# A two-part kernel on one core: VectorE takes attention taps in pairs, and a second input is loaded in four pieces

## The chip, the cores and the metric

The program runs on one core of a Trainium2 chip. A core has engines that work side by side, each with its own queue of instructions, taken strictly in order: TensorE (PE; weight loads are listed apart as PEld), VectorE (DVE), ScalarE (ACT), GpSimd (POOL) and SyncE (SP), which here issues nearly all DMAs. The engines wait for each other through semaphores. SBUF is the working memory of 128 partitions, PSUM takes the results of TensorE. The metric is the device time of one execution, in microseconds (us); less is better.

## The reference

Two independent computations on (1, 2048, 448) bf16 inputs, their results side by side in an output of (1, 2048, 896). Part A is a diagonal complex state-space model with 448 states, part B is windowed attention with 16 heads of 28, in which each token looks at itself and at 7 earlier tokens at distances of 2, 4, ... 14.

```python
# A
Lam_bar = jnp.exp(dt * Lam)
B_bar = ((Lam_bar - 1.0) / Lam)[:, None] * Bmat
Bu = jnp.einsum("bld,pd->blp", x + 0j, B_bar)
for t in range(L):
    h = Lam_bar[None, :] * h + Bu[:, t, :]
    hs.append(h)
y = 2.0 * jnp.einsum("blp,dp->bld", hseq, Cmat).real + x * Dskip[None, None, :]
# B, W = 8, dil = 2
qkv = x @ wqkv
kg, vg = k[:, :, idx_c, :], v[:, :, idx_c, :]     # idx = pos - 2 * [0..7]
logits = jnp.einsum("bhsd,bhswd->bhsw", q, kg) * scale     # masked where idx < 0
attn = softmax(logits)
out = einsum("bhsw,bhswd->bhsd", attn, vg) @ wo
```

## The kernel before

**Layout.** 2048 positions are 128 chunks of 16 consecutive tokens: partition p holds chunk p, and "token j" (0 to 15) stands for 128 positions at once. All work is per token j.

**Part B.** x is loaded from the last tokens to the first. For each j TensorE transposes x (`pt_x`), ScalarE copies that out into `xT` (which lies in the memory that `vd` takes later), and TensorE projects to q, k or v (`qkv_ps`, 4 matmuls of 448 columns each); ScalarE or VectorE evicts it to `qd`, `kd`, `vd`. `kd` and `vd` have 14 halo rows in front, which SyncE fills by copies from the partition before (`_halo`), with zeros for the first chunk (`_zero`). The logits are made by VectorE in two blocks b of 8 tokens (b = 1, tokens 8-15, first). For each of 8 taps w it multiplies `qd` by the shifted `kd` (`prod`, 3584 elements a partition), adds the upper half of the 28 head elements to the lower (`prod` again, 1792) and once more (`sd`, 896). TensorE then sums the remaining 7 slices with 7 identity matmuls into `lg_ps`; after 4 taps ScalarE copies them to `logits`. The softmax has a `top` on VectorE (the maximum), a subtraction on TensorE, an exponential on ScalarE and a `bottom` on VectorE. Then P.V on VectorE, in three blocks of tokens (8-15, 0-5, 6-7): per tap a product of `attn` with the shifted `vd` and an add into one of two sums. Each token's sums are transposed by TensorE (`pt_o`), copied by ScalarE (`oT_sb`), multiplied by `wo` (`wo_ps`), copied (`yb`) and stored.

**Part A.** B_bar is turned into `Bcat` by TensorE and ScalarE. x of A is loaded, transposed (`pt_x`, line 751) and kept in `xaT_sb`. Level 1 is a recurrence over the 16 tokens in two halves, `l1A` and `l1B`, on TensorE with an eviction by ScalarE behind each step; the states go out to `hs` in DRAM. Level 2 is a chain of 7 steps over the 128 chunks (line 829), again TensorE and ScalarE in turn. Then `ga`, and for each token the corrections `coA`, `coB` and the output `y_ps` (4 matmuls at line 902, 7 at line 907).

**Order.** Nothing is ordered by hand. Each piece of work is a unit with an engine, a cost, dependences and a priority; `Planner.run` simulates the engines with these costs, starts at each point the unit that can start earliest (ties by priority), and writes the instructions out in that order. So the order on each engine is fixed when the program is built, and a unit that is late on the chip holds up all that stand behind it on its engine. Some units may go to either of two engines (evictions of projections to ScalarE, or to VectorE at a handicap `HAND`). `acq` and `rel` name buffers that a unit takes and gives back: 4 PSUM banks `mm`, 2 `pt`, 2 `lg`, `SD` buffers `sd`.

B's x and then A's x lie in one place, tag `xin`: the first load of A's x can only be issued when all 16 transposes of B have been read. V of tokens 0 to `VH` - 1 is held: its projections may not start before the last step of `l1A`.

Of the kernel before, what the change touches and what calls it, by code (L numbers as in the profile page):

```python
# [15 lines left out]
D = 448  # L16
# [20 lines left out]
SD = 2  # L37
VH = 8
PVP = (4, 5, 6)
WIDE = set()  # L40
# [8 lines left out]
def act(n):  # L49
    return n / 1200.0 + 0.06  # L50
# [6 lines left out]
def vec2(n):  # L57
    return n / 1920.0 + 0.15
# [85 lines left out]
class PartB:  # L144
    JG = (3, 2, 1, 0)
    HAND = (0.5, 1.0, 1.0)
    PV = ((1, 8, 16, "xin", 2), (0, 0, 6, "qd", 2), (0, 6, 8, "lg", 2))
# [6 lines left out]
    def loads(self):  # L154
        nc, pool, P = self.nc, self.pool, self.plan
        self.x_sb = pool.tile([NCH, T, D], bf16, name="xb_sb", tag="xin")
# [5 lines left out]
        def xload(j0, j1):  # L162
            nc.sync.dma_start(self.x_sb[:, j0:j1], xv[:, j0:j1])
# [22 lines left out]
    def alloc(self):  # L186
# [6 lines left out]
        self.zsrc = pool.tile([1, DH * H], bf16, name="zsrc")  # L193
        V.memset(self.zsrc[:], 0.0)
# [45 lines left out]
    def prep(self):  # L240
# [4 lines left out]
        self.lgb, self.lps = {}, {}  # L245
        self.attn = None
        P.add("SP", 0.1, lambda: self._zero(self.kd), prio=0)
        for g in self.JG:
            if g < 3 and g > 0:
                self.q_proj(range(4 * g + 4, 4 * g + 8), 0)  # L250
            for j in range(4 * g + 3, 4 * g - 1, -1):
                box = {}

                def tr(j=j, box=box):
                    pt = box["pt"] = self.psum.tile([KP, KT, NCH], bf16, name="pt_x", tag="pt")
                    for k in range(KT):
                        nc.tensor.transpose(pt[:, k, :], self.x_sb[:, j, k * KP:(k + 1) * KP], self.ident[:])
# [44 lines left out]
    def qk(self, b, prio):  # L302
# [4 lines left out]
        for w in range(W):  # L307
            o = HALO + j0 - DIL * w

            nd = 14 if (b, w) in WIDE else 7  # L310

            def mul(w=w, o=o, i0=0, i1=JB):
                if "pr" not in box:
                    box["pr"] = pool.tile([NCH, DH, JB, H], bf16, name="prod", tag="prod")
                V.tensor_tensor(box["pr"][:].rearrange("p d j h -> p j d h")[:, i0:i1], self.qd[:, j0 + i0:j0 + i1],  # L315
                                self.kd[:, o + i0:o + i1], op=ALU.mult)

            split = b == 1 and w == 0

            def prod(w=w, o=o, nd=nd, split=split, mul=mul):  # L320
                mul(i0=0, i1=HB if split else JB)
                pr = box.pop("pr")
                prf = pr[:].rearrange("p d j h -> p d (j h)")
                sd = box[w] = pool.tile([NCH, nd, BH], bf16, name="sd", tag="sd", bufs=SD)
                if nd == 14:
                    V.tensor_tensor(sd[:], prf[:, 0:14], prf[:, 14:28], op=ALU.add)
                else:
                    V.tensor_tensor(prf[:, 0:14], prf[:, 0:14], prf[:, 14:28], op=ALU.add)  # L328
                    V.tensor_tensor(sd[:], prf[:, 0:7], prf[:, 7:14], op=ALU.add)  # L329

            def summ(w=w, nd=nd):
                if w % 4 == 0:
                    box["lps"] = self.psum.tile([NCH, 4, BH], f32, name="lg_ps", tag="lg")
                for d in range(nd):
                    nc.tensor.matmul(box["lps"][:, w % 4, :], lhsT=self.ident[:], rhs=box[w][:, d, :],  # L335
                                     start=(w % 4 == 0 and d == 0), stop=(d == nd - 1), skip_group_check=True)
                if w % 4 == 3 and (b, w // 4) in self.maskrow:
                    nc.tensor.matmul(box["lps"][:].rearrange("p w (j h) -> p w j h", h=H), lhsT=self.ident[:],
                                     rhs=self.maskrow[b, w // 4].unsqueeze(3).to_broadcast([NCH, 4, JB, H]),
                                     start=False, stop=True, skip_group_check=True)  # L340

            def evict(w=w):
                if w == 3:
# [3 lines left out]
                nc.scalar.copy(self.lgb[b][:, w - 3:w + 1, :], box["lps"][:])  # L347
            deps = [self.u_q[j] for j in range(j0, j0 + JB)]
            deps += [self.u_kh[p] if p < HALO else self.u_k[p - HALO] for p in range(o, o + JB)]
            cost = vec2(3584) + vec2(1792) + (vec2(896) if nd == 7 else 0.0)  # L350
            if split:
                cost -= vec2(1792) - 0.15
                deps = [P.add("DVE", vec2(1792), lambda mul=mul: mul(i0=HB), deps[HB:JB] + deps[JB + HB:], prio)] + deps
            u = P.add("DVE", cost, prod, deps, prio, acq="sd", lat=0.15 if w % 4 == 3 else 0.8)
            ds.append(u)
            sums.append(P.add("PE", pe(nd, 128) + (0.21 if w % 4 == 3 else 0.0), summ, [u] + sums[-1:], 2, rel="sd",
                              acq="lg" if w % 4 == 0 else None))
            if w % 4 == 3:
# [666 lines left out]
```

## Time and profile before

| | |
|---|---|
| time, median of 3 runs | 163.42 us (162.52 to 164.99) |
| the profiled execution | 163.71 us, its span 161.9 us |
| TensorE busy | 153.8 us (95% of the span), 1748 matmuls |
| VectorE busy | 141.8 us (88%), 156 instructions |
| ScalarE busy | 118.8 us (73%), 242 instructions |
| DMA engines busy | 46% (main queue) |
| granted TensorE clock | 0.996 of full speed |

The span runs from the first instruction to the last on the core; the execution's own time has 1.8 us more around it. Busy time counts the whole length of an instruction, and matmuls overlap, so a busy TensorE isn't TensorE at its peak. In a timeline each row has the start, the length, the engine, the line of the kernel, the operation, and what it writes and reads; a bracket at its end gives the time that the engine was idle before it and who released it. Line numbers are those of the kernel before.

### The profile page before, as it was taken

Reading aid. Unit: us, or ns where it says so; the run is one execution under the profiler, and the core shown is the slowest. Engines: PE = TensorE matmul, PEld = TensorE weight load, DVE = VectorE, ACT = ScalarE, POOL = GpSimd, SP = SyncE. Lnnn points to the kernel's source line nnn. Section 1 sums busy time; section 2 is a strip of 40 time slices with the busy share of each in tenths; the row PEclk is TensorE's granted clock in tenths of the full one; section 3 lists DMA queues with packets and bytes.
Section 4 is the critical chain, followed back from the end, with each engine's and each line's share of the span. In section 5 each row is a group of like instructions: output and inputs, shape, how many; then the busy total and the mean of one; then the engine's idle time right before and its main releaser. Section 6 shows DMA issues by size and latency. Waiting matters only on the chain.

```text
span 161.9 us, 4322 instructions
## 1 busy us (share of the span) xinstructions
PE 153.8 (95%) x1748; PEld 116.5 (72%) x1748; DVE 141.8 (88%) x156; ACT 118.8 (73%) x242; POOL 4.8 (3%) x36
## 2 busy tenths in 40 slices
PE   7998999999999899998999899999999999999991
PEld 7655575767999798998997556677776676786760
DVE  1479999999999999999999999999999999999800
ACT  3497899999976778555557799856657686676862
POOL 5004000000000020000000000000000000000000
PEclk9999999999999999999999999999999999999998
DMA  5999233596875623122222440755543334511312
GB/s 156 327 304 222 61 112 91 158 332 148 117 133 184 174 93 110 63 89 84 89 85 59 136 116 5 218 168 156 167 120 114 113 106 125 170 59 61 115 59 85
DMA packets 24147, 21.39 MB, mean 132 GB/s; under 512 B 9259, under 2 KB 22469, under 8 KB 24127
## 3 DMA queue, kind: packets, MB, share of 16 engines
q1 hardware_dynamic: 24056, 21.11, 46.0%
q8 instruction: 13, 0.21, 0.6%
q14 instruction: 7, 0.06, 0.1%
q10 hardware_dynamic: 71, 0.01, 0.0%
HBM read 10.56 MB, written 7.34 MB: 111 GB/s over the span
## 4 chain that ended last, share of the span: by engine, by line
PE 50%; DVE 33%; ACT 13%; issue 2%; DVEq 0%; ACTq 0%
DVE prod L315 16%; PE y_ps L907 13%; PE qkv_ps L221 10%; DVE prod L328 9%; PE wo_ps L451 7%; DVE sd L329 5%; PE pt_o L441 5%; ACT vd L260 3%; PE warm L963 2%; ACT kd L229 2%; PE coA L884 2%; PE coA L886 2%; PE y_ps L902 2%; ACT Bcat L728 2%; ACT pbuf L834 2%; PE coB L884 2%
## 5 line engine op out<-in xcount | busy, mean ns | idle before, releaser
L221 PE MATMUL qkv_ps<-wqkv_nat,vd 112*128 112x448 bf16 x192 | 41.4, 355 | 1.1 <-ACT vd L260 0.7
L315 DVE TENSOR_TENSOR prod<-qd,kd 128x3584 bf16<-128x3584 bf16 (+1 forms) x17 | 32.5, 1912 | 0.7
L221 PEld LDWEIGHTS <-vd 112*128 112x128 bf16 x192 | 17.8, 98 | 15.0 <-issue 1.6
L794 PEld LDWEIGHTS <-Bcat 112*128 112x128 bf16 x448 | 26.6, 98 | 1.1
L425 DVE TENSOR_TENSOR acc<-acc,pv_tmp 128x3584 bf16<-128x3584 bf16 (+2 forms) x18 | 25.2, 1402 | 0.6
L424 DVE TENSOR_TENSOR pv_tmp<-attn,vd 128x3584 bf16<-128x3584 bf16 (+2 forms) x18 | 25.2, 1400 | 0.4
L907 PE MATMUL y_ps<-Ccat,ht 128*128 128x448 bf16 x112 | 24.5, 352 | 0.0
L328 DVE TENSOR_TENSOR prod<-prod 128x1792 bf16<-128x1792 bf16 x16 | 17.5, 1092 | 0.5
L794 PE MATMUL l1A<-xaT_sb,Bcat 112*128 112x128 bf16 x256 | 16.9, 219 | 0.0
L912 ACT CAST ya<-y_ps 128x448 bf16<-128x448 f32 x16 | 8.5, 532 | 10.2 <-PE y_ps L907 7.7
L907 PEld LDWEIGHTS <-ht 128*128 128x128 bf16 x112 | 10.0, 97 | 6.8
L805 ACT CAST ht<-l1A 128x512 bf16<-128x512 f32 x15 | 8.8, 586 | 7.3 <-PE l1A L801 6.4
L451 PE MATMUL wo_ps<-wo_p,oT_sb 112*128 112x448 bf16 x64 | 13.4, 352 | 0.0
L794 PE MATMUL l1B<-xaT_sb,Bcat 112*128 112x128 bf16 x192 | 13.4, 219 | 0.0
L399 ACT CAST yb<-wo_ps 128x448 bf16<-128x448 f32 x16 | 8.5, 532 | 6.2 <-PE wo_ps L451 5.4
L884 PEld LDWEIGHTS <-ident 128*128 128x128 bf16 x112 | 11.0, 98 | 0.5
L329 DVE TENSOR_TENSOR sd<-prod 128x896 bf16<-128x896 bf16 x16 | 10.0, 625 | 1.5
L335 PE MATMUL lg_ps<-sd,ident 128*128 128x128 bf16 x112 | 8.9, 219 | 2.1 <-DVE sd L329 2.1
L890 ACT CAST ht<-coA 128x512 bf16<-128x512 f32 x16 | 10.1, 631 | 0.0
L451 PEld LDWEIGHTS <-oT_sb 112*128 112x128 bf16 x64 | 6.1, 97 | 5.3
L229 ACT CAST vd<-qkv_ps 128x448 bf16<-128x448 f32 x16 | 9.0, 575 | 1.4 <-PE qkv_ps L221 1.2
L805 ACT CAST ht<-l1B 128x384 bf16<-128x384 f32 x15 | 7.3, 484 | 3.6 <-PE l1B L801 3.3
(135 smaller groups left out, 272.7 us busy)
## 6 DMA issues: line engine op xcount, KB each, us to landing
hin<-hs SPq DMA_DIRECT2D x16, 224.0 KB, 3.2
hs<-ht SPq DMA_DIRECT2D x15, 128.0 KB, 1.9
xa_sb<-in_A_x_dram SPq DMA_DIRECT2D x4, 448.0 KB, 5.4
out_dram<-ya SPq DMA_DIRECT2D x16, 112.0 KB, 1.7
out_dram<-yb SPq DMA_DIRECT2D x16, 112.0 KB, 1.9
hs<-ht SPq DMA_DIRECT2D x15, 96.0 KB, 1.9
xb_sb<-in_B_x_dram SPq DMA_DIRECT2D x3, 448.0 KB
wqkv_nat<-in_B_wqkv_dram SPq DMA_DIRECT2D x3, 392.0 KB, 4.7
```

What stands on the lines that cost most here:

```text
L221: nc.tensor.matmul(ps[:].rearrange("p h d -> p (h d)"), lhsT=self.xT[:, j // 4, k, j % 4, :], rhs=self.wn[:, k, which].rearrange("p h d -> ...
L229: nc.scalar.copy(out(), box["ps"])
L315: V.tensor_tensor(box["pr"][:].rearrange("p d j h -> p j d h")[:, i0:i1], self.qd[:, j0 + i0:j0 + i1], self.kd[:, o + i0:o + i1], op=ALU.mult)
L328: V.tensor_tensor(prf[:, 0:14], prf[:, 0:14], prf[:, 14:28], op=ALU.add)
L329: V.tensor_tensor(sd[:], prf[:, 0:7], prf[:, 7:14], op=ALU.add)
L424: V.tensor_tensor(tmp[:], aa, vv, op=ALU.mult)
L425: V.tensor_tensor(acc[:, g], acc[:, g], tmp[:], op=ALU.add)
L451: nc.tensor.matmul(ps[:], lhsT=jb["oT"][:, kt, :], rhs=self.wo_p[:, kt, :], start=(kt == 0), stop=(kt == KT - 1))
L794: nc.tensor.matmul(ps[:, m - m0, :], lhsT=self.Bcat[:, k, m, :], rhs=self.xT[:, j, k, :], start=(j == 0 and k == 0 and m == m0), stop=(j = ...
L805: nc.scalar.copy(slot(j)[:, m0:m1, :], box[h][:])
L884: nc.tensor.matmul(ps[:, m - m0, :], lhsT=self.ident[:], rhs=self.hins[:, j % 3, m, :], start=(m == m0), stop=False, skip_group_check=True)
L907: nc.tensor.matmul(jb["y"][:], lhsT=self.hts[:, j % 3, m, :], rhs=self.Ccat[:, m, :], start=False, stop=(m == NM - 1), skip_group_check=True)
```

## The change

Six things change together, and the planner then writes a new order on all engines.

- The taps of the logits go in pairs. Two products are written to one `prod` tile of twice the size, and one add of 3584 elements and one of 1792 fold both. TensorE then runs 14 identity matmuls. There is one `sd` buffer of twice the size, where there were two.
- P.V goes in pairs as well: two products to `pv_tmp`, and one add of both into the two sums. The sums of the first two blocks lie in the place of `kd`.
- B's x has four tiles of four tokens, and A's x is loaded to the same four places, last group of B first; each load waits only for that group's transposes.
- Transposes of B's x get a higher priority (`TRP`), k of tokens 0-7 a lower one (`KPR`).
- V of tokens 0-11 is held for the last step of `l1A`, before it was 0-7.
- The planner's cost of a VectorE instruction has 0.19 us as its fixed part, before it was 0.15.

```diff
-SD = 2
-VH = 8
+SD = 1
+FOUR = set()
+TRP = (-0.2, -0.2, -0.2, 0)
+KPR = (0.6, 0.6, 0, 0)
+XAP = 0
+VH = 12
 def vec2(n):
-    return n / 1920.0 + 0.15
+    return n / 1920.0 + 0.19
...
-        self.x_sb = pool.tile([NCH, T, D], bf16, name="xb_sb", tag="xin")
+        self.x_sb = [pool.tile([NCH, 4, D], bf16, name="xb_sb", tag="xin" + str(g)) for g in range(4)]
...
-        self.nc.sync.dma_start(t_[0:1, 0:HALO].rearrange("o j d h -> o j (d h)"),
-                               self.zsrc[:].unsqueeze(1).to_broadcast([1, HALO, DH * H]))
+        nz = HALO * D // NCH
+        self.nc.sync.dma_start(t_[0:1, 0:HALO].rearrange("o j d h -> o (j d h)").rearrange("o (n c) -> o n c", c=NCH),
+                               self.wz[0:1].unsqueeze(1).to_broadcast([1, nz, NCH]))
...
-                u = P.add("PE", pe(4, 128), tr, [self.u_x[j]], 0 if g > 1 else 0.3, acq="pt")
+                u = P.add("PE", pe(4, 128), tr, [self.u_x[j]], TRP[g], acq="pt")
...
-                self.u_xe[j] = P.add("ACT", act(512), ev, [u], 0, rel="pt")
-                u, e = self._proj_unit(j, 1, 0 if g > 1 else 0.6, (), lambda j=j: self.kd[:, HALO + j], hand=self.HAND[0])
+                self.u_xe[j] = P.add("ACT", act(512), ev, [u], TRP[g], rel="pt")
+                u, e = self._proj_unit(j, 1, KPR[g], (), lambda j=j: self.kd[:, HALO + j], hand=self.HAND[0])
...
+        for pair in range(W // 2):
+            w0 = 2 * pair
+            nd = 4 if (b, pair) in FOUR else 7
+            muls = []
+            for i in range(2):
+                w = w0 + i
+                o = HALO + j0 - DIL * w
+
+                def mul(i=i, o=o, i0=0, i1=JB):
+                    if "pr" not in box:
+                        box["pr"] = pool.tile([NCH, 2, DH, JB, H], bf16, name="prod", tag="prod")
+                    V.tensor_tensor(box["pr"][:, i].rearrange("p d j h -> p j d h")[:, i0:i1],
+                                    self.qd[:, j0 + i0:j0 + i1], self.kd[:, o + i0:o + i1], op=ALU.mult)
...
+            def fold(pair=pair, nd=nd):
+                prf = box.pop("pr")[:].rearrange("p w d j h -> p w d (j h)")
+                sd = box["sd"] = pool.tile([NCH, 2, 7, BH], bf16, name="sd", tag="sd", bufs=SD)
+                V.tensor_tensor(prf[:, :, 0:14], prf[:, :, 0:14], prf[:, :, 14:28], op=ALU.add)
+                V.tensor_tensor(sd[:], prf[:, :, 0:7], prf[:, :, 7:14], op=ALU.add)
...
-                evs.append(P.add("ACT", act(512), evict, sums[-4:], 2))
+                evs.append(P.add("ACT", act(512), evict, sums[-2:] + self.u_top, 2))
...
-                self.lg[b] = pool.tile([NCH, W, BH], f32, name="expo", tag="lg", bufs=2)
+                self.lg[b] = pool.tile([NCH, W, BH], f32, name="expo", tag="lg")
...
+    def _acc(self, j0, n):
+        if n < 3:
+            return self.pool.tile([NCH, 2, n, DH, H], bf16, name="acc", tag="lg")
+        if self.accs is None:
+            self.accs = self.pool.tile([NCH, 2, 14, DH, H], bf16, name="acc", tag="kd")
+        o = 0 if j0 >= JB else JB
+        return self.accs[:, :, o:o + n]
...
-        for g in range(2):
-            for i in range(4):
-                w = g * 4 + i
+        for i in range(4):
+            for g in range(2):
+                w = 2 * i + g
...
-                    if i == 0:
-                        V.tensor_tensor(acc[:, g], aa, vv, op=ALU.mult)
-                    else:
-                        tmp = pool.tile([NCH, n, DH, H], bf16, name="pv_tmp", tag="prod")
-                        V.tensor_tensor(tmp[:], aa, vv, op=ALU.mult)
-                        V.tensor_tensor(acc[:, g], acc[:, g], tmp[:], op=ALU.add)
+                    if i > 0 and g == 0:
+                        box["tmp"] = pool.tile([NCH, 2, n, DH, H], bf16, name="pv_tmp", tag="prod")
...
+                    V.tensor_tensor((box["tmp"] if i else box["acc"])[:, g], aa, self.vd[:, o:o + n], op=ALU.mult)
...
+            if i > 0:
+                def add():
+                    V.tensor_tensor(box["acc"][:], box["acc"][:], box["tmp"][:], op=ALU.add)
+                last = P.add("DVE", vec2(2 * n * D), add, [last], prio - 0.01, rel="prod")
...
+        for g in range(4):
+            dd = [deps[j] for j in range(4 * (3 - g), 4 * (3 - g) + 4)]
+            self.u_x.append(P.add("SP", dma(458752), lambda g=g: go(g), dd, XAP, lat=2.5))
```

More of the change, by code (lines that the diff above doesn't have):

```diff
@@ L346, in evict @@
                 self.lps[b].append(box["lps"])
[L347 to L354, printed above, removed]
+                nc.scalar.copy(self.lgb[b][:, w0 - 2:w0 + 2, :], box["lps"][:])
+            u = P.add("DVE", vec2(3584) + vec2(1792) + (vec2(768) if nd == 4 else 0.0) + 0.1, fold, muls, prio - 0.01,
+                      acq="sd", rel="prod", lat=0.15)
             ds.append(u)
[L356 to L359 removed]
+            sums.append(P.add("PE", pe(2 * nd, 128) + (0.21 if w0 % 4 == 2 else 0.0), summ, [u] + sums[-1:], 2,
+                              rel="sd", acq="lg" if w0 % 4 == 0 else None))
+            if w0 % 4 == 2:
+                evs.append(P.add("ACT", act(512), evict, sums[-2:] + self.u_top, 2))
         self.u_lg[b], self.u_d[b] = evs, ds
@@ L950 @@
     ps = _Ps()
-    plan = Planner({**BUFS, "sd": SD, "oT": 3, "yb": 2, "ya": 2})
+    plan = Planner({**BUFS, "sd": SD, "prod": 1, "oT": 3, "yb": 2, "ya": 2})
     ctx.enter_context(tc.manual_schedule())
```

94 lines of the change are left out of this document (40 added, 54 removed).

## The prediction

> **What bounds the kernel now.** I read the page first (busy times, chain), then busy time by stretch, then the chain in order of time, then the timelines of VectorE, ScalarE and SyncE.
>
> ```profile
> PE 153.8 (95%) x1748; PEld 116.5 (72%) x1748; DVE 141.8 (88%) x156; ACT 118.8 (73%) x242; POOL 4.8 (3%) x36
> PE 50%; DVE 33%; ACT 13%; issue 2%; DVEq 0%; ACTq 0%
> ```
>
> ```profile
> 10.00:20.00 10.00, 9.34 (x62) 5.24 (x61) 9.35 (x26) 8.25 (x16) 1.71 (x4) 1.00 0.76 163
> 30.00:40.00 10.00, 10.00 (x102) 7.19 (x101) 9.39 (x8) 10.00 (x24) 0.00 (x0) 1.00 0.84 239
> 90.00:100.00 10.00, 9.57 (x84) 6.10 (x84) 9.76 (x12) 9.14 (x22) 0.00 (x0) 1.00 0.30 87
> 140.00:150.00 10.00, 10.00 (x106) 7.13 (x104) 9.76 (x12) 6.41 (x14) 0.00 (x0) 1.00 0.27 91
> ```
>
> The second fence is busy time by stretch: after the length stand PE, PEld, DVE, ACT and POOL. TensorE and VectorE are both full, and ScalarE is full from 30 to 40. The chain puts 33% on VectorE, but with two full engines a chain can pass through either. So I measure TensorE by its work, from the chain in order of time (start, length, what):
>
> ```profile
> 4.37 0.53 PE warm L963 x5
> 8.55 4.56 PE qkv_ps L221 x24
> 90.08 0.55 PE lg_ps L335 x7
> 90.63 0.22 PE lg_ps L338
> 102.27 0.22 PE coB L884
> 129.64 0.90 PE pt_o L441 x16
> 149.86 1.51 PE wo_ps L451 x8
> 155.46 0.20 PE y_ps L902 x4
> 157.94 0.58 PE y_ps L907 x3
> ```
>
> A matmul of 448 columns costs 0.1895 us (1.51 / 8), of 128 columns 0.0557 (0.89 to 0.90 / 16), of 112 columns 0.05, a 512-wide one 0.215, a warm-up 0.107. The program has 368, 1243, 92, 7 and 36 of them, and 2 small ones: 69.7 + 69.2 + 4.6 + 1.5 + 3.9 + 0.3 = 149.2 us of work. I call time minus work already queued ahead the **lag**. At 90.08 the queue holds 83.4 us ahead: lag 6.6. At 102.27 it holds 93.5: lag 8.8. At the end (157.94 + 0.58 = 158.5) it is 158.5 - 149.2 = 9.3. So TensorE loses almost nothing after 102, and the change cannot shorten that part; it has no fewer matmuls either (its queue also adds to 149.2). Only a smaller lag brings the end forward.
>
> The Trainium skill ("Trainium Kernel Development and Optimization", Performance Expectations) calls matmul busy time a bad measure and weight-load busy a good one; by it TensorE is at 72% and the end would follow VectorE. The constant steps above disagree.
>
> **Where the lag arises.**
>
> ```profile
> PE lg_ps L335 <- DVE sd L329: 2.1, 4, 0.8
> 14.21 1.69 PE L221 MATMUL qkv_ps<-wqkv_nat,vd 112*128 112x448 bf16 x8 [0.66 <-ACT vd L260]
> 96.97 0.92 PE L221 MATMUL qkv_ps<-wqkv_nat,vd 112*128 112x448 bf16 x4 [0.34 <-ACT vd L229]
> 101.88 0.33 PE L854 MATMUL ga<-pbuf,Pmat 128*128 128x128 bf16 x3 [0.16 <-ACT Ga L859]
> ```
>
> Four waits on VectorE's folded taps (2.1), one on ScalarE's transposes at 14, and from 90 to 102 the level-2 chain, which lifts the lag from 6.6 to 8.8.
>
> **Taps in pairs (logits).** Start and length of VectorE's instructions:
>
> ```profile
> 42.63 2.02 DVE L315 TENSOR_TENSOR prod<-qd,kd 128x3584 bf16<-128x3584 bf16 x1
> 44.69 1.09 DVE L328 TENSOR_TENSOR prod<-prod 128x1792 bf16<-128x1792 bf16 x1
> 45.89 0.62 DVE L329 TENSOR_TENSOR sd<-prod 128x896 bf16<-128x896 bf16 x1
> 46.55 2.02 DVE L315 TENSOR_TENSOR prod<-qd,kd 128x3584 bf16<-128x3584 bf16 x1
> 58.24 0.42 DVE L370 TENSOR_TENSOR mx<-logits 128x512 bf16<-128x512 bf16 x1
> 59.16 2.02 DVE L315 TENSOR_TENSOR prod<-qd,kd 128x3584 bf16<-128x3584 bf16 x1
> 62.95 0.69 DVE L386 TENSOR_TENSOR sm<-expo 128x512 f32<-128x512 f32 x1
> 66.59 2.02 DVE L315 TENSOR_TENSOR prod<-qd,kd 128x3584 bf16<-128x3584 bf16 x1
> 108.63 2.02 DVE L421 TENSOR_TENSOR acc<-attn,vd 128x3584 bf16<-128x3584 bf16 x1
> 110.56 2.02 DVE L424 TENSOR_TENSOR pv_tmp<-attn,vd 128x3584 bf16<-128x3584 bf16 x1
> 112.62 2.02 DVE L425 TENSOR_TENSOR acc<-acc,pv_tmp 128x3584 bf16<-128x3584 bf16 x1
> 122.79 1.55 DVE L421 TENSOR_TENSOR acc<-attn,vd 128x2688 bf16<-128x2688 bf16 x1
> 124.26 1.55 DVE L424 TENSOR_TENSOR pv_tmp<-attn,vd 128x2688 bf16<-128x2688 bf16 x1
> 125.85 1.56 DVE L425 TENSOR_TENSOR acc<-acc,pv_tmp 128x2688 bf16<-128x2688 bf16 x1
> ```
>
> One tap takes 46.55 - 42.63 = 3.92, two 7.84. A pair becomes two products, one fold of 3584 and one of 1792. The step from one instruction to one that reads its result is 2.06 (42.63 to 44.69), to one that does not 1.93 (108.63 to 110.56). The gap behind the first fold is 0.11 (44.69 + 1.09 to 45.89). So a pair takes 1.93 + 2.06 + (2.02 + 0.11) + (1.09 + 0.07) = 7.28: 0.56 less. The fixed part of an instruction is 2 x 1.09 - 2.02 = 0.16 by these rows.
>
> The Trainium skill ("VectorE: DVE Perf Modes", the section on the TRN2 errata) gives 58 cycles + elements / 2 at 0.96 GHz, so a fixed part of 0.06 us; 1.927 for 3584 elements agrees with the step of 1.93 but not with the 2.06 behind a dependence. By it a pair would save only 0.12, close to rival C.
>
> One `sd` and one `prod` buffer: the next `sd` is written some 6 us after the last, TensorE's 14 matmuls on it take 0.8. That cover goes only if TensorE comes over 5 us late. `prod` is written and read by VectorE alone: nothing. The zero rows from `wz` (the same 12 KB in smaller pieces), the single `expo` buffer (its second use is some 30 us behind the first) and the sums in `kd`'s place (VectorE read that last) cost nothing for the same reason: the order already holds them apart.
>
> **Front: A's x in four pieces, priorities of transposes and k.**
>
> ```profile
> 25.82 0.34 SPq L738 DMA_DIRECT2D xa_sb<-in_A_x_dram  x1
> 39.77 2.65 SPq L507 DMA_DIRECT2D cn<-in_A_C_re_dram  x4
> 11.33 0.26 ACT L601 ACTIVATE tmp<-tmp 128x91 f32<-128x91 f32 x1
> 13.13 0.54 ACT qd L231
> 21.47 0.96 ACT vd L260 x2
> 27.68 0.87 ACT kd L229 x2
> ```
>
> All B transposes now come before the eight k of groups 1 and 0. Laying ScalarE's new queue end to end from 11.6 (its sine ends there) with 0.48 a transpose, 0.44 a k and 0.54 a q, the last k ends near 28.5, and TensorE enters its run of 36 matmuls at 21.1 with 18.9 us of work done: lag 2.2, where before it was 2.8 already at 14.21 (11.4 done). One k moves from VectorE to ScalarE (0.44). From there ScalarE is the bound until the x of A is transposed (10.00 of 10 in 30 to 40), so the gain is what it idled in 10 to 20 (1.75), less 0.44: about 1.2 us. A's x is issued from about 10 instead of 25.8; its transposes stand behind the 36 matmuls, and nobody waits for it: nothing won by itself. In SyncE's queue the four loads now stand ahead of halo copies and wait for transposes; the halos of k are first read by the third pair, after 38, some 15 us later: nothing. The C loads (eight issues, from 39.77) and `wo` move forward too; TensorE is full from 40 to 50, so nothing. Bounds for the front: 0 to 2 us.
>
> VectorE here: the second half product needs q of token 8, evicted near 23.3, and tap 1 k of token 6, near 24.2. So the first pair's `sd` ends at 23.4 + 1.05 + 2.06 + 2.13 + 1.09 = 29.7, with one Pmat build (2688 elements, so 1.5) still to come.
>
> **Who waits for whom in the taps.** `sd` ready against TensorE's work ahead of it in the new queue: pair 0: 29.7, 27.7; pair 1: 37.2, 34.6; pair 2 (behind Pmat): 45.9, 43.3; pair 3: 53.2, 50.5. Pair 4 carries the maximum (58.24 to 59.16, and some 0.7 of waiting for the logits' eviction): 62.1, 59.2. Behind the softmax (62.95 to 66.59, 3.6): 73.0, 70.5; 80.3, 77.2; 87.6, 84.7. The differences are 2.0 to 3.1. So VectorE allows a lag of 3 at the end of the taps where before it was 6.6; TensorE's own small losses (the 512-wide ones, ScalarE in 30 to 40) make it 3.6.
>
> **V of tokens 0-11 held.** Four more V units (0.76 us of TensorE each) lie inside level 2, between its steps, and four fewer in level 1, whose two halves cover each other (60 to 90 lose only on `sd`). ScalarE has 9.14 of 10 in 90 to 100; each unit brings it 0.44 and TensorE 0.76, so it gets looser. I take +1.8 instead of +2.2 for level 2 (bounds 1.0 and 4): lag 5.4 on leaving it. The price is on VectorE: V of tokens 8, 6 and 4 is evicted near 88, 89.7 and 92.5, and the first three products of P.V want them at 87.6, 89.5 and 91.7: about 1.6 us of waiting.
>
> **P.V in pairs.** For tokens 8-15: six steps of 1.93, two of 2.06, three adds of 7168 elements (2 x 2.02 - 0.16 = 3.88; steps 3.8, 3.8, 3.9) = 27.2, the softmax between them 4.6 (maximum 0.95, rest 3.6), and two products of the next block that the new order puts in (2 x 1.47): 87.6 + 27.2 + 4.6 + 2.9 + 1.6 = 123.9. TensorE's queue has 117.9 us ahead of the first `pt_o`, 4.0 more than before (nearly two more tokens of A): it gets there at 117.9 + 5.4 = 123.3. So it waits 0.6: lag 6.0. Tokens 0-5 follow with six products (1.47 and 1.6 in turn), three adds of 5376 elements (2 x 1.55 - 0.16 + 0.04 = 3.0) and two small products (1.0): 123.9 + 19.2 = 143.1, reached at 137.5 + 6.0 = 143.5. Tokens 6-7 are ready near 150, reached at 152.8. No further wait. The new queue ends in four groups of projections with one bare wait on ScalarE's eviction of the last: 0.3.
>
> **Sum.** The lag falls from 9.3 to 6.3: 3.0 us. Of the profiled execution (span 161.9, 163.7 in all) 160.7 is left; its runs have a median of 163.42, 0.3 under it. I forecast 160.5. Two per cent, about what a measurement of this kernel tells from no change, is 3.3 us: the forecast lies just on that edge.
>
> **Rivals.**
>
> A, the engines fit better than I laid them (front gains 2, V waits nothing, level 2 loses 1): lag 4.4, 158.8. For it: the sums above leave VectorE 0.5 to 1 of slack in the taps. Against: six near ties in a row, where each miss adds and no hit gives back. 0.2.
>
> B, ties go wrong: VectorE reaches pairs or P.V 1 to 2 us later, and TensorE, whose order is fixed, stands at `lg_ps` or `pt_o`: 161.7 to 163. 0.27.
>
> C, the pairs do not do what they say: an instruction of twice the elements takes the time of two, so a pair stays at 7.84 and an add of 7168 elements at 4.04. Pair 7 then comes 7 x 0.56 = 3.9 later and P.V 0.5 more: 165. Against: 2.02 is less than 2 x 1.09, and a product step of 1.93 is on record. 0.08. The rule quoted above (0.12 a pair) would give 163.7 or so.
>
> D, slower: the held V. If ScalarE's level-2 evictions go ahead of V's, or the exponential stands behind them, the products of tokens 8-15 start late; every microsecond past 123.3 delays `pt_o`, and 31.4 us of TensorE's work behind it, one for one. From 3 us beyond my 123.9 the kernel is no faster; at 7 (130.9) it takes 167.7. For it: 9.14 of 10 on ScalarE. Against: twelve V need 5.3 us of ScalarE in about 15. 0.1.
>
> **Chances.** My forecast 0.35 (159.6 to 161.6), A 0.2, B 0.27, C 0.08, D 0.1. Faster by over 2% (below 160.15): A and somewhat more than half of the forecast's cases, 0.4. Slower by over 2% (above 166.7): nearly all of D, 0.1. Within: 0.5. The range leaves out the best end of A and most of D: 158.2 to 164.2.
>
> **What would show it.** Right: four waits on `sd` gone or under 1 us in all; a pair at 7.3 from first product to the next pair's; A's x issued from 10 on; the last `sd` near 87.5, level 2 left and the first `coA` reached near 98, TensorE's end near 155.5. Wrong: pair steps near 7.8; a long wait of `pt_o` on `acc`, or of `acc` on `vd`; ScalarE idle in 20 to 40 as before; a level 2 that adds over 2.5 of lag.

## The result, and the profile after

The kernel after takes 160.92 us (median of 6 runs, 160.53 to 161.17); the kernel before, run beside it, 163.6 us. The ratio is 0.985, with a 95% interval of 0.982 to 0.988: it is faster by 1.5%, less than the 2% that the prediction took for the least change a measurement can tell, but the interval leaves out 1. Medians are over all runs; a ratio compares means and leaves out the few runs in the chip's slower state. The forecast was 160.5 us, range 158.2 to 164.2. The profiled execution takes 161.04 us (span 159.2), before it was 163.71 (161.9).

One sentence of the description ahead of the prediction is wrong: the priorities of k (`KPR`) hold the values that stood in the code before, so k of tokens 0-7 is not put lower; only the transposes (`TRP`) change theirs.

The page of the kernel after, busy time and the shares of the chain:

```profile
PE 152.4 (96%) x1748; PEld 115.6 (73%) x1748; DVE 135.9 (85%) x129; ACT 119.0 (75%) x243; POOL 4.8 (3%) x36
PE 71%; ACT 13%; DMA 7%; DVE 5%; issue 1%; SPq 1%; ACTq 0%
```

VectorE does 129 instructions where it did 156, and 5.9 us less. The chain now goes through VectorE for 5% only, where it was 33%; among TensorE's waits it is left only at the warm-up. Busy time by stretch of the kernel after (length, then PE, PEld, DVE, ACT, POOL, the granted clock, DMA share, GB/s):

```profile
10.00:20.00 10.00, 10.00 (x79) 6.27 (x78) 9.16 (x26) 9.93 (x23) 1.72 (x4) 1.00 1.10 250
30.00:40.00 10.00, 9.68 (x89) 6.36 (x87) 9.86 (x7) 10.00 (x24) 0.00 (x0) 1.00 0.58 107
90.00:100.00 10.00, 9.48 (x89) 6.28 (x88) 9.79 (x12) 9.87 (x23) 0.00 (x0) 1.00 0.41 118
140.00:150.00 10.00, 10.00 (x105) 7.12 (x103) 7.26 (x10) 6.64 (x14) 0.00 (x0) 1.00 0.18 59
```

From 10 to 20 ScalarE rises from 8.25 to 9.93 and TensorE from 9.34 to 10.00: that is the front. From 30 to 40 ScalarE is the bound (10.00), from 90 to 100 TensorE still has gaps (9.48) around level 2. At the end VectorE has spare time (9.76 before, 7.26 now). The timeline of VectorE after (start, length, instruction; a bracket is the idle time before it and who ended it):

```profile
37.37 3.95 DVE L321 TENSOR_TENSOR prod<-qd,kd 128x3584 bf16<-128x3584 bf16 x2
41.35 2.03 DVE L332 TENSOR_TENSOR prod<-prod 128x3584 bf16<-128x3584 bf16 x1
43.48 1.09 DVE L333 TENSOR_TENSOR sd<-prod 128x1792 bf16<-128x1792 bf16 x1
44.61 3.96 DVE L321 TENSOR_TENSOR prod<-qd,kd 128x3584 bf16<-128x3584 bf16 x2
...
85.53 1.09 DVE L333 TENSOR_TENSOR sd<-prod 128x1792 bf16<-128x1792 bf16 x1
86.81 3.96 DVE L430 TENSOR_TENSOR acc<-attn,vd 128x3584 bf16<-128x3584 bf16 x2 [0.19 <-ACT vd L231]
...
117.63 3.89 DVE L436 TENSOR_TENSOR acc<-acc,pv_tmp 128x7168 bf16<-128x7168 bf16 x1
```

A pair takes 44.61 - 37.37 = 7.24 us. The last `sd` is ready at 85.53 + 1.09 = 86.62, the sums of tokens 8-15 at 121.52. In the waits of the kernel after (engine, line, awaited, us in total, times, longest) no row of `lg_ps` on `sd` is left; the largest wait of TensorE behind the warm-up is for the copy ahead of `wo_ps`:

```profile
PE wo_ps L460 <- ACT oT_sb L410: 0.5, 2, 0.3
```

**Where the time came from.** The lag (time minus matmul work ahead, with the prediction's prices of one matmul) at marks along TensorE's queue, worked out in the same way from the trace of each kernel. The names are those of the experiments below; e5, e6 and e8 have the order of the kernel after up to the first `coB`.

| kernel | at 12 us | last `sd` | `ga` | first `coB` | first `pt_o` | end | work ahead of the first `coB` |
|---|---|---|---|---|---|---|---|
| before | 2.0 | 6.6 | 7.5 | 8.8 | 8.8 | 9.3 | 93.5 |
| after | 1.5 | 3.2 | 3.2 | 4.8 | 5.5 | 6.6 | 95.9 |
| e1, before, plan's cost 0.19 | 1.9 | 4.0 | 4.9 | 6.8 | 7.9 | 8.5 | 95.9 |
| e2, after, plan's cost 0.15 | 1.7 | 3.0 | 3.4 | 4.6 | 5.2 | 5.8 | 93.5 |
| e3, after, V of 0-7 held | 1.3 | 3.1 | 3.1 | 5.4 | 8.6 | 8.9 | 97.3 |
| e4, after, old front | 1.9 | 4.3 | 4.3 | 6.2 | 6.5 | 7.6 | 93.5 |
| e5, after, folds split | 1.9 | 3.6 | 3.6 | 5.2 | 6.1 | 6.8 | 95.9 |
| e6, after, adds split | 2.1 | 3.8 | 3.8 | 5.4 | 6.6 | 7.5 | 95.9 |
| e7, pairs of the logits alone | 2.1 | 4.6 | 5.5 | 7.0 | 9.9 | 10.4 | 97.3 |
| e8, after, all sums joined | 1.9 | 3.6 | 3.6 | 5.2 | 5.9 | 10.4 | 95.9 |
| e9, single taps | 1.5 | 4.5 | 4.9 | 6.3 | 6.7 | 7.3 | 93.5 |
| e10, as e3, three `ya` | 2.3 | 4.2 | 4.3 | 6.6 | 9.2 | 9.5 | 97.3 |
| e11, before, V of 0-11 held | 1.5 | 6.4 | 6.5 | 7.9 | 8.7 | 9.3 | 95.9 |
| e12, as e2, first sums joined | 2.0 | 3.4 | 3.8 | 5.0 | 5.2 | 7.7 | 93.5 |

After against before: 3.4 us are won up to the last `sd`, 0.6 more up to the first `coB`; 0.6 are given back from there to `pt_o`, and 0.7 in the last stretch. What is left is 2.7, and that is the difference of the two profiled executions. Each row is one execution. The lag at 12 us differs by up to 1.0 us between kernels whose order is the same there (e3 and e10; after, e5, e6 and e8 have 1.5 to 2.1), and the difference is still there at the last `sd`. So 0.5 of the 3.4 us most likely belongs to the start of these two executions, not to the change, and a difference of half a microsecond between two rows shows nothing by itself.

### The profile page after: what moved, and what is told of

The parts are those of the page before. It is cut to its first block, busy times and chain, and to the rows that moved or that the text cites. A ratio compares the mean times of both kernels' runs of the same rounds, so it can differ in the third digit from the quotient of the medians.

```text
span 159.2 us, 4285 instructions
## 1 busy us (share of the span) xinstructions
PE 152.4 (96%) x1748; PEld 115.6 (73%) x1748; DVE 135.9 (85%) x129; ACT 119.0 (75%) x243; POOL 4.8 (3%) x36
## 4 chain that ended last, share of the span: by engine, by line
PE 71%; ACT 13%; DMA 7%; DVE 5%; issue 1%; SPq 1%; ACTq 0%
PE qkv_ps L223 14%; PE y_ps L921 12%; PE l1A L808 9%; PE l1B L808 7%; PE wo_ps L460 6%; DMA wqkv_nat<-in_B_wqkv_dram 4%; ACT xaT_sb L768 3%; PE lg_ps L342 3%; PE pt_o L450 3%; DVE prod L321 3%; DMA out_dram<-yb 2%; PE l1A L815 2%; ACT qd L233 2%; PE y_ps L916 2%; PE coA L900 2%; PE coA L898 2%
## 5 line engine op out<-in xcount | busy, mean ns | idle before, releaser
L223 PE MATMUL qkv_ps<-wqkv_nat,vd 112*128 112x448 bf16 x192 | 40.4, 352 | 0.3 <-DMA wqkv_nat<-in_B_wqkv_dram 0.2
L321 DVE TENSOR_TENSOR prod<-qd,kd 128x3584 bf16<-128x3584 bf16 (+1 forms) x17 | 32.0, 1911 | 1.2 <-ACT qd L233 0.9
L430 DVE TENSOR_TENSOR pv_tmp<-attn,vd 128x3584 bf16<-128x3584 bf16 (+2 forms) x18 | 24.4, 1396 | 0.1
L436 DVE TENSOR_TENSOR acc<-acc,pv_tmp 128x7168 bf16<-128x7168 bf16 (+2 forms) x9 | 23.8, 2647 | 0.3
L332 DVE TENSOR_TENSOR prod<-prod 128x3584 bf16<-128x3584 bf16 x8 | 16.2, 2025 | 0.3
L768 ACT COPY xaT_sb<-pt_x 112x512 bf16<-112x512 bf16 x16 | 10.1, 742 | 0.0
L231 ACT CAST kd<-qkv_ps 128x448 bf16<-128x448 f32 x16 | 8.3, 539 | 2.2 <-PE qkv_ps L223 2.2
L410 ACT CAST oT_sb<-pt_o 112x512 bf16<-112x512 f32 x16 | 8.6, 593 | 1.5 <-PE pt_o L450 1.5
```

What stands on the lines that cost most here:

```text
L223: nc.tensor.matmul(ps[:].rearrange("p h d -> p (h d)"), lhsT=self.xT[:, j // 4, k, j % 4, :], rhs=self.wn[:, k, which].rearrange("p h d -> ...
L321: V.tensor_tensor(box["pr"][:, i].rearrange("p d j h -> p j d h")[:, i0:i1], self.qd[:, j0 + i0:j0 + i1], self.kd[:, o + i0:o + i1], op=AL ...
L332: V.tensor_tensor(prf[:, :, 0:14], prf[:, :, 0:14], prf[:, :, 14:28], op=ALU.add)
L410: (self.nc.scalar.copy if eng == "ACT" else self.nc.vector.tensor_copy)(out, in_)
L430: V.tensor_tensor((box["tmp"] if i else box["acc"])[:, g], aa, self.vd[:, o:o + n], op=ALU.mult)
L436: V.tensor_tensor(box["acc"][:], box["acc"][:], box["tmp"][:], op=ALU.add)
```

## The experiments

None of them leaves out a part of the reference. Times are compared through their ratios to the kernel before, run beside them; those have a 95% interval.

### One part undone at a time

**e4: the front as before.** The transposes' priorities and the single wait of A's x come back; four places stay.

```diff
-TRP = (-0.2, -0.2, -0.2, 0)
+TRP = (0.3, 0.3, 0, 0)
-self.u_xe[j] = P.add("ACT", act(512), ev, [u], TRP[g], rel="pt")
+self.u_xe[j] = P.add("ACT", act(512), ev, [u], 0, rel="pt")
-dd = [deps[j] for j in range(4 * (3 - g), 4 * (3 - g) + 4)]
+dd = list(deps.values())
```

> The changed kernel with the front as it was: A's x waits for all 16 transposes of B's x, old priorities of the transposes. Theory: TensorE and VectorE are each about 1 to 1.5 us later when the taps begin, nothing later makes up for it; 161.9 to 162.5. Rival (the taps are bound by VectorE's own work, the front hidden): 160.7 to 161.2.

161.99 us, ratio 0.991 (0.987 to 0.995), as expected: the front is worth 0.6% or 1.0 us, near the prediction's 1.2. The interval touches that of the kernel after (0.982 to 0.988), so the size is rough. In the trace one wait of the kernel before, at 14 us, is back, which the kernel after has not:

```profile
PE qkv_ps L223 <- ACT vd L263: 0.7, 1, 0.7
```

From 12 us to the last `sd` the lag grows by 2.4, in the kernel after by 1.7, so 0.7 of it is seen there.

**e9: the taps of the logits one by one**, in the kernel after with cost 0.15 (160.23 us, e2 below). P.V stays in pairs.

```diff
-    return n / 1920.0 + 0.19
+    return n / 1920.0 + 0.15
-SD = 1
+SD = 2
-for pair in range(W // 2):
+for w in range(W):
...
-V.tensor_tensor(prf[:, :, 0:14], prf[:, :, 0:14], prf[:, :, 14:28], op=ALU.add)
-V.tensor_tensor(sd[:], prf[:, :, 0:7], prf[:, :, 7:14], op=ALU.add)
+V.tensor_tensor(prf[:, 0:14], prf[:, 0:14], prf[:, 14:28], op=ALU.add)
+V.tensor_tensor(sd[:], prf[:, 0:7], prf[:, 7:14], op=ALU.add)
```

> The kernel after with the taps of the logits one by one as in the kernel before (two buffers of 896 elements, cost 0.15 in the plan); front, A's x, the held V of 0-11 and P.V in pairs stay. Theory (the pair counts through the moment at which VectorE has a tap ready): the last sd comes 7 x 0.60 = 4.2 us later than 86.6, near 90.8, and TensorE's new queue has 85.0 us of work ahead of it, so the lag there is at least 5.8 instead of 3.2; with the 2.8 us that follow in the run with cost 0.15 the lag at the end is 8.6: 162.7 to 163.4 us, waits on sd of 2 us or more, P.V of tokens 8-15 near 125.7. Rival (held V and front carry the gain, and the order hides late taps as it did when only the cost was raised to 0.19): 160.2 to 161.5.

162.35 us, ratio 0.995 (0.992 to 0.997); e2 has 0.981 (0.978 to 0.983). So the pairs are worth some 2.3 us here. The first fence is a row of VectorE's timeline in e2, the second one of e9's, the third the waits of e9:

```profile
83.98 1.09 DVE L333 TENSOR_TENSOR sd<-prod 128x1792 bf16<-128x1792 bf16 x1
```

```profile
88.82 0.62 DVE L333 TENSOR_TENSOR sd<-prod 128x896 bf16<-128x896 bf16 x1
```

```profile
PE lg_ps L339 <- DVE sd L333: 1.2, 3, 0.6
```

The last `sd` is ready at 89.44 instead of 85.07, and with 85.0 us of work ahead the lag is 4.5 there. The expectation took its start from the kernel after (86.62) and not from e2, so its lag of 8.6 at the end is 1.5 us too high, and the time lies 0.4 us under its range. From 85.07, its own steps give 85.07 + 4.2 - 85.0 + 2.8 = 7.1 at the end, and 7.3 was measured. Of the 4.4 us that the `sd` comes later, 1.6 are time by which it was early in e2 and 1.3 are covered by more work ahead. The other 1.5 or so are in the lag at once and still there at the end: from there on a late tap is paid one for one, as the prediction said. (The two profiled executions differ by 1.8 us: the 1.5, and 0.3 outside the span, whose cause is open.)

**e3: V of tokens 0-7 held, as before.**

```diff
-VH = 12
+VH = 8
```

> The changed kernel with V of tokens 0-7 held, as before the change, not 0-11. Theory: four V units (3.0 us of TensorE) leave level 2 and no longer fill its waits for ScalarE; level 2 added 0.6 us of lag in the changed kernel and 2.2 before; time 161.5 to 162.5. Rival (the held V costs more by VectorE's waits for it than it fills): 160.2 to 160.8.

163.65 us, ratio 1.001 (0.998 to 1.003). That is a miss of over a microsecond: with this number alone the whole gain is gone. Up to `ga` nothing is lost (lag 3.1). From there to the first `coB` the lag grows by 2.3 instead of 1.6, which is what the expectation looked for (level 2 without its fillers); but most goes from the first `coB` to `pt_o` (5.4 to 8.6). Busy time by stretch there, first of the kernel after, then of e3 (the last two columns are the DMA share and GB/s):

```profile
100.00:104.00 4.00, 3.77 (x42) 2.54 (x38) 4.00 (x2) 2.32 (x5) 0.00 (x0) 1.00 0.38 120
108.00:112.00 4.00, 4.00 (x48) 3.04 (x47) 3.97 (x2) 2.19 (x6) 0.00 (x0) 1.00 0.47 156
```

```profile
100.00:104.00 4.00, 3.27 (x34) 2.12 (x32) 4.00 (x2) 1.94 (x5) 0.00 (x0) 1.00 0.00 0
108.00:112.00 4.00, 2.69 (x28) 1.68 (x27) 3.97 (x2) 1.49 (x4) 0.00 (x0) 1.00 0.48 147
```

From 108 to 112 TensorE is idle for a third of the time and ScalarE for more than half: something else is awaited. From 100 to 104 no DMA moves at all. SyncE's waits from 88 to 116, in the kernel after and then in e3:

```profile
SPq L888 <- PE coB L898: 2.7, 1, 2.7
```

```profile
SPq L888 <- PE coB L900: 6.5, 3, 4.9
```

SyncE's timeline at the first two reloads of states, after and then in e3:

```profile
101.13 0.81 SPq L888 DMA_DIRECT2D hin<-hs  x2
```

```profile
103.15 1.98 SPq L888 DMA_DIRECT2D hin<-hs  x2
```

The DMA issues of A's output in the kernel after (KB each, median us to landing), two rows of ScalarE's timeline in e3, and one piece of e3's chain:

```profile
out_dram<-ya SPq DMA_DIRECT2D x16, 112.0 KB, 1.7
```

```profile
108.00 0.53 ACT L926 CAST ya<-y_ps 128x448 bf16<-128x448 f32 x1 [0.64 <-DMA out_dram<-ya]
111.42 0.53 ACT L926 CAST ya<-y_ps 128x448 bf16<-128x448 f32 x1 [2.51 <-DMA out_dram<-ya]
```

```profile
106.83 4.50 DMA out_dram<-ya
```

Line 888 loads the states of one token into one of three places (`hin`). The fourth load has to wait until `coA` and `coB` of the first token have read theirs. In e3 the first `coB` stands at 97.3 us of work in TensorE's queue, after at 95.9, so the loads start at 103.15 instead of 101.13. The stores of A's output go through the same queue between the loads: one of them takes 4.50 us to land, where the median of those stores after is 1.7. (Why it is slow stays open: in the kernel after a store also stands between loads, at 106.30, and lands in 1.7.) With two `ya` buffers ScalarE stands for 2.51 us, and TensorE behind it.

**e10: e3 with a third buffer for A's output.** The order on every engine is the same as in e3.

```diff
-jb["ya"] = pool.tile([NCH, D], bf16, name="ya", tag="ya", bufs=2)
+jb["ya"] = pool.tile([NCH, D], bf16, name="ya", tag="ya", bufs=3)
```

> The kernel after with V of 0-7 held (163.65 us as measured) and three buffers of A's output tile instead of two; the order on every engine is the same as in that run. Theory (stores of A's output that land late, behind loads of the states that were issued together, hold ScalarE and through it TensorE): the waits of ScalarE on that store (3.2 us between 96 and 126) go, TensorE gets back most of the 2.3 us that followed from them: 161.2 to 162.5. Rival (the first coB, and with it the next load of the states, stands too late in TensorE's queue; the stores are only where it shows): 163 to 163.8.

163.09 us, ratio 0.997 (0.994 to 1.000): 0.6 us less than e3, not clear of noise, at most half of what the theory expected, and within the rival's range. ScalarE's waits on these stores are gone from the list, but another has come in TensorE's waits:

```profile
PE coA L898 <- DMA hin<-hs: 1.2, 1, 1.2
```

So the store was where a part of the loss showed, not its cause. And part of the loss waits for no DMA at all. Two rows of TensorE's timeline in e3:

```profile
103.74 0.74 PE L921 MATMUL y_ps<-Ccat,ht 128*128 128x448 bf16 x3 [0.57 <-ACT ht L904]
105.10 0.22 PE L898 MATMUL coB<-hin,ident 128*128 128x128 bf16 x1 [0.28 <-ACT ya L926]
```

In the planner's order these stand directly behind the work whose result ScalarE first has to copy. By 106.07 the lag has grown by 1.3 us (5.4 to 6.7), and by as much at the same place in e10 and e7; in the kernel after the first of these waits costs 0.4. The remaining 2.0 us in e3, 1.4 in e10 and 1.6 in e7 fall where loads and stores are awaited.

What remains as the cause is the order with its late `coB`: bare waits on ScalarE, then the late restart of the state loads. For that speaks the last column of the table. The lag that is added between the first `coB` and the first `pt_o` goes with the place of that `coB`: 0.1 to 0.6 us in the five kernels that have it at 93.5, 0.7 to 1.1 in the six at 95.9, and 2.6 to 3.2 in the three at 97.3. No run moved this one unit and left the rest in place, so the cause is inferred from this agreement.

**e11: the held V alone, in the kernel before.**

```diff
-VH = 8
+VH = 12
```

> The kernel before with one number changed: V of tokens 0-11 held instead of 0-7. Theory (holding V saves in the output start only what the bunched loads of the states cost, and before has no such loss: its lag grows by 0.1 from the first coB to the first pt_o): no gain; VectorE's products of tokens 8-15 want V of 8, 6 and 4 and wait, and pt_o has only 113.8 us of work ahead, so it is 0 to 1.5 us late: 163.3 to 165. Rival (the held V is worth 2.6 us by itself, as after against the run with 0-7 held): 160.8 to 161.5.

163.67 us, ratio 1.002 (1.000 to 1.005): nothing, as the theory expected. TensorE's waits in e11:

```profile
PE lg_ps L335 <- DVE sd L329: 2.3, 4, 0.9
PE pt_o L441 <- DVE acc L425: 0.2, 1, 0.2
```

The four waits on `sd` are those of the kernel before (2.1 there), and the first `coB` even moves back from 93.5 to 95.9. So holding more V has no worth of its own. It is worth 2.6 us (1.6%) in the kernel after, probably because the plan without it puts `coB` late.

**e7: the pairs of the logits alone.** The kernel after with V of 0-7 held, cost 0.15, the old front (the edits of e4) and the adds of P.V split as in e6. The places of x and of the sums, the order of P.V's products and the single `sd` buffer stay those of the kernel after.

```diff
-    return n / 1920.0 + 0.19
+    return n / 1920.0 + 0.15
-VH = 12
+VH = 8
```

> The kernel before plus the pairs of the logits alone: front old, V of 0-7 held, planner's cost 0.15, adds of P.V not paired. Theory: the last sd comes near 87 instead of 90 and TensorE's waits for it go, 1.3 to 2.2 us of the 2.7 gained; 161.4 to 162.3. Rival order: 163.2 to 163.8.

164.77 us, ratio 1.007 (1.003 to 1.010): 0.7% slower than before, outside the expectation and outside its rival. The pairs do what they should up to the last `sd` (lag 4.6 instead of 6.6), and then the same place takes 2.9 us, as in e3, with the first `coB` again at 97.3. One stretch of e7, in which TensorE works for 3.15 of 4 us and ScalarE for half:

```profile
104.00:108.00 4.00, 3.15 (x33) 2.06 (x32) 4.00 (x3) 1.98 (x5) 0.00 (x0) 1.00 0.35 68
```

### What the pair saves on VectorE

**e5: products in pairs, the folds tap by tap.**

```diff
-V.tensor_tensor(prf[:, :, 0:14], prf[:, :, 0:14], prf[:, :, 14:28], op=ALU.add)
-V.tensor_tensor(sd[:], prf[:, :, 0:7], prf[:, :, 7:14], op=ALU.add)
+for i in range(2):
+    V.tensor_tensor(prf[:, i, 0:14], prf[:, i, 0:14], prf[:, i, 14:28], op=ALU.add)
+    V.tensor_tensor(sd[:, i], prf[:, i, 0:7], prf[:, i, 7:14], op=ALU.add)
```

> The changed kernel in its own order, but each pair's two folds are issued tap by tap (four adds where there are two). Theory (TensorE's lag; VectorE counts only where its folded taps come last): a pair goes from 7.25 us back to about 7.75, the last sd comes 3.5 to 4 us later than 86.6, TensorE's wait there grows by 2.0 to 2.8, time 163.0 to 163.8. Rival order (the gain comes from the planner's corrected cost, so from the order alone): 160.9 to 161.2, the order is unchanged. Rival VectorE (the end follows VectorE): all of it, 164.5 to 165.

161.18 us, ratio 0.985 (0.982 to 0.988), the same as after: the expectation failed, because a pair hardly gets longer. For the same reason the run says nothing for its rival, that the gain lies in the order alone. VectorE's timeline in e5:

```profile
38.07 3.96 DVE L321 TENSOR_TENSOR prod<-qd,kd 128x3584 bf16<-128x3584 bf16 x2
41.94 1.08 DVE L333 TENSOR_TENSOR prod<-prod 128x1792 bf16<-128x1792 bf16 x1
43.13 0.62 DVE L334 TENSOR_TENSOR sd<-prod 128x896 bf16<-128x896 bf16 x1
43.67 1.08 DVE L333 TENSOR_TENSOR prod<-prod 128x1792 bf16<-128x1792 bf16 x1
44.79 0.62 DVE L334 TENSOR_TENSOR sd<-prod 128x896 bf16<-128x896 bf16 x1
45.45 2.03 DVE L321 TENSOR_TENSOR prod<-qd,kd 128x3584 bf16<-128x3584 bf16 x1
```

Six instructions take 45.45 - 38.07 = 7.38; four take 7.24; two single taps took 7.84, also with six. So merging the folds saves 0.14 of the 0.60, and 0.46 comes from the order: the fold of one tap can now stand behind an instruction whose result it doesn't read. From a fold to the `sd` that reads it is 43.13 - 41.94 = 1.19 (the second time 1.12); from an `sd` to the fold of the other tap is 43.67 - 43.13 = 0.54, which is less than the 0.62 that the `sd` lasts. The Trainium skill ("VectorE: DVE Perf Modes", the section on the TRN2 errata) has a fixed part of 58 cycles, 0.06 us, in an instruction; for single operations the same section notes that about 150 were measured, 0.16 us. Two instructions fewer for 0.14 us agree with the 58; the 0.60 of a pair agrees with neither, since most of it isn't a fixed part.

**e6: the adds of P.V split in two.**

```diff
-V.tensor_tensor(box["acc"][:], box["acc"][:], box["tmp"][:], op=ALU.add)
+for g in range(2):
+    V.tensor_tensor(box["acc"][:, g], box["acc"][:, g], box["tmp"][:, g], op=ALU.add)
```

> The changed kernel in its own order, but each of the nine paired adds of P.V is issued as two (18 adds as before the change). It costs VectorE 9 x 0.16 = 1.4 us, 0.5 of it ahead of the first pt_o, where VectorE is 2 us early (121.5 against 123.55). Theory: nothing, 160.7 to 161.2. Rival VectorE: 162.2 to 162.5. Rival order: nothing.

161.11 us, ratio 0.987 (0.984 to 0.989), as expected. VectorE's rows in e6:

```profile
99.76 3.95 DVE L437 TENSOR_TENSOR acc<-acc,pv_tmp 128x3584 bf16<-128x3584 bf16 x2
103.63 1.55 DVE L430 TENSOR_TENSOR acc<-attn,vd 128x2688 bf16<-128x2688 bf16 x1
```

The same place in the kernel after:

```profile
99.11 3.88 DVE L436 TENSOR_TENSOR acc<-acc,pv_tmp 128x7168 bf16<-128x7168 bf16 x1
102.91 1.55 DVE L430 TENSOR_TENSOR acc<-attn,vd 128x2688 bf16<-128x2688 bf16 x1
```

Two adds step on after 103.63 - 99.76 = 3.87 us, one of twice the size after 3.80: again 0.07 us for one instruction less. VectorE has room in this stretch, and the time shows nothing of it.

### What the plan's cost changes

**e1 and e2.** The fixed part in the planner's cost of a VectorE instruction, first raised in the kernel before, then put back in the kernel after. In e1:

```diff
-    return n / 1920.0 + 0.15
+    return n / 1920.0 + 0.19
```

In e2:

```diff
-    return n / 1920.0 + 0.19
+    return n / 1920.0 + 0.15
```

> The kernel before with one constant changed: the planner's fixed part of a VectorE instruction 0.19 instead of 0.15, so a new order, no instruction changed. Theory: the taps still take 7.84 a pair and the last sd still comes near 90, but TensorE gets other work ahead of it, the four waits on sd (2.1) shrink to under 1; 162.3 to 163.2. Rival order: 160.9 to 161.5.

> The changed kernel with the planner's fixed part of a VectorE instruction at its old 0.15, so a new order, no instruction changed. With 0.15 a planned pair is 7.23 us, with 0.19 7.39; the trace shows 7.25. Theory: no loss, 160.5 to 161.4. Rival order: back to 162.5 to 163.6.

e1 takes 163.53 us, ratio 0.998 (0.995 to 1.001): no gain shown, less than the expectation had (162.3 to 163.2), though its waits on `sd` vanish from the list. The last `sd` of e1:

```profile
89.52 0.62 DVE L329 TENSOR_TENSOR sd<-prod 128x896 bf16<-128x896 bf16 x1
```

It is ready at 90.1, as late as before (90.0). But the plan puts 86.2 instead of 83.4 us of work ahead of it, and the lag there falls from 6.6 to 4.0 without any faster VectorE. From there to `pt_o` it grows by 3.9, where before it grew by 2.2, so most of the gain is spent by the time the outputs come (0.8 is left at the end of this execution). e2 takes 160.23 us, ratio 0.981 (0.978 to 0.983), 0.3 us under the expected range: no loss, so the gain does not hang on the cost, and if anything better than after (0.982 to 0.988), with the first `coB` back at 93.5. The two intervals overlap, so this is not settled.

### Looking for a better version

**e8: VectorE joins all sums ahead of `pt_o`.** TensorE's work falls from 149.2 to 145.7 us.

```diff
-PV = ((1, 8, 16, 2), (0, 0, 6, 2), (0, 6, 8, 2))
+PV = ((1, 8, 16, 1), (0, 0, 6, 1), (0, 6, 8, 1))
```

> The changed kernel, where VectorE adds the two sums of each P.V block before TensorE transposes them: 64 matmuls of 128 columns fewer (3.6 us of TensorE's work), three adds more on VectorE (1.9 + 1.4 + 0.5, 3.8 us with gaps, 2.0 of them ahead of the first pt_o, where it has 2.0 to spare). Theory (TensorE's work and lag set the end): 157.3 to 158.5. Rival VectorE: 163 to 165.

161.21 us, ratio 0.987 (0.982 to 0.992): 3.5 us of matmuls less, and no gain; the theory's range is missed, and so is the rival's. A row of TensorE's waits, and the end of VectorE's timeline, in e8:

```profile
PE wo_ps L460 <- ACT oT_sb L410: 3.0, 5, 1.0
```

```profile
151.31 0.62 DVE L440 TENSOR_TENSOR acc<-acc 128x896 bf16<-128x896 bf16 x1
```

VectorE ends at 151.9 instead of 147.5. The last tokens then come after A's outputs are used up, and `wo_ps` has nothing to run while ScalarE copies `oT_sb`. The lag rises from 5.9 to 10.4.

**e12: only the sums of tokens 8-15 joined, with cost 0.15.**

```diff
-PV = ((1, 8, 16, 2), (0, 0, 6, 2), (0, 6, 8, 2))
+PV = ((1, 8, 16, 1), (0, 0, 6, 2), (0, 6, 8, 2))
-    return n / 1920.0 + 0.19
+    return n / 1920.0 + 0.15
```

> The kernel after with cost 0.15 in the plan (160.23 us as measured) and the two sums of tokens 8-15 added by VectorE before pt_o, those of tokens 0-7 left apart. TensorE's work falls from 149.2 to 147.4 us. Theory (lag): VectorE has 8-15 ready at 122.2 + 2.0 = 124.2, TensorE gets there at 120.2 + 5.2 = 125.4 and doesn't wait; tokens 0-5 are ready near 143.3, reached near 143.2; the lag at the end stays near 6: 158.5 to 159.2. Rival (as with all sums joined, VectorE's end and the short chain of pt_o, oT and wo at the end take it back): 159.9 to 160.8.

159.91 us, ratio 0.979 (0.976 to 0.982). That is the lowest median of all, but it misses the theory's 158.5 to 159.2, lies at the lower end of the rival's range, and can't be told from e2. TensorE's timeline in e12:

```profile
144.94 1.69 PE L460 MATMUL wo_ps<-wo_p,oT_sb 112*128 112x448 bf16 x8 [0.23 <-ACT oT_sb L410]
147.75 1.71 PE L460 MATMUL wo_ps<-wo_p,oT_sb 112*128 112x448 bf16 x8 [0.23 <-ACT oT_sb L410]
150.62 1.69 PE L460 MATMUL wo_ps<-wo_p,oT_sb 112*128 112x448 bf16 x8 [0.26 <-ACT oT_sb L410]
153.47 1.69 PE L460 MATMUL wo_ps<-wo_p,oT_sb 112*128 112x448 bf16 x8 [0.26 <-ACT oT_sb L410]
```

In all four last groups the wait is bare, where after has it bare in two groups in all (0.5 us). With each of the four the lag grows by 0.4. In the traces that takes back the 1.8 us of matmuls saved: from `pt_o` to the end the lag grows by 2.5, in e2 by 0.6. e2 and e12 both beat the kernel before by about 2%. Against the kernel after (0.982 to 0.988) the interval of e12 overlaps at its edge only, that of e2 a little more, so a gain over it is likely and not shown.

## Why the prediction was right, and where it was not

The time (160.92 for 160.5) and its mechanism, a smaller lag at unchanged matmul work, were right; the times of rivals A (158.8), B (161.7 to 163) and D (163.7 and more) were not met. That the total came out so close is partly luck, as the terms below show. Step by step:

| step | forecast | measured |
|---|---|---|
| first pair's `sd` | 29.7 | 28.7 |
| a pair | 7.28 | 7.24 |
| last `sd` ready | 87.6 | 86.6 |
| front | 1.2 us | 1.0 by time, 0.7 by lag (e4) |
| lag at the last `sd` | 3.6 | 3.2 |
| lag on leaving level 2 | 5.4 | 4.8 (first `coB`) |
| first `coA` | near 98 | 96.5 |
| V waits of VectorE | 1.6 | 0.2 |
| sums of 8-15 ready, first `pt_o` reached | 123.9, 123.3 | 121.5, 123.4 |
| from `pt_o` to the end | 0.3 | 1.1 |
| lag at the end | 6.3 | 6.6 |
| TensorE's end | 155.5 | 155.8 |

- **VectorE.** All its times came out about a microsecond early, from the first pair on. The add of 7168 elements lasts 3.89 for 3.88. Rival C (the pairs don't save) is out, and with it the 163.7 by the quoted rule: a pair is 7.24. But the step "the fixed part of an instruction is 0.16" was wrong as an explanation. It took the difference of two durations for what merging saves; e5 shows 0.07 an instruction (0.14 / 2), e6 the same, and the other 0.46 a pair come from independent neighbours. The number was right because the steps were read from rows that held both.
- **V held.** This was the worst-sized step. The prediction gave the edit 0.4 us (level 2 at +1.8 instead of +2.2) and charged 1.6 us to VectorE. VectorE waits 0.2: V of token 8 was there at 86.8 and not near 88. And the worth is 2.6 us (e3), mostly in a place that the prediction took for safe: it wrote that TensorE loses almost nothing after 102. That holds in the order of the kernel before, where the lag grows by 0.1 from the first `coB` to `pt_o`. In the order that the planner writes with the pairs and 0-7 held it grows by about 3 (e3, e7). Why is inferred, not shown. Rival D looked for the danger in holding V; the danger lay in not holding it.
- **Output start and tail.** P.V was 2.4 us earlier than forecast, so the 0.6 us of waiting for it did not come. In its place 0.7 us are lost between `coB` and `pt_o`. The tail costs 1.1 instead of 0.3: at each of the two bare waits on `oT_sb` the lag steps up by 0.4 to 0.5 (5.5 to 6.0 near 134 us, 6.0 to 6.4 near 153), though the rows of the waits have only 0.5 for both. In the terms of the sum the misses are -0.4 (up to the last `sd`), -0.2 (level 2), +0.1 (to `pt_o`) and +0.8 (tail); they cancel to 0.3. The first is about the 0.5 by which the profiled execution started better than that of the kernel before.
- **Parts don't add.** The prediction added the gains of the edits. The runs say: pairs alone +0.7%, held V alone +0.2%, all together -1.5%; all but the held V 0.0%. The planner writes the whole order anew each time, and a part is worth what the new order makes of it.

## What to carry to other kernels

Measure the bound engine by its work and follow the lag along its queue; it says where an edit wins and where that is lost again, which busy shares do not (TensorE's weight-load share is 71 to 73% in all these kernels, while the time goes from 159.9 to 164.8). Where a planner or scheduler writes the order, compare the queue of the new program with the old one also far behind the place of the edit, above all the first reader that frees a ring of buffers and the work that stands directly behind the result that it reads, since an order that wins 2 us ahead can lose 3 there (e7). On VectorE, put instructions next to each other that don't read each other's results before merging them.

## What the runs showed of the hardware

- On VectorE an instruction behind the one whose result it reads starts later: in e5 the `sd` starts 1.19 and 1.12 us behind a fold of 1.08 us that it reads, and an independent fold 0.54 us behind an `sd` of 0.62. So an independent instruction can start before the one ahead has ended by the profile.
- A store of 112 KB, of a kind that lands in 1.7 us in the median, took 4.50 between loads of 224 KB each (e3), though in the kernel after another one between such loads took 1.7. One more buffer moved the wait to the loads (1.2 us in e10) and gave some 0.6 us, not clear of noise.
